# Attention beside a spectral mixing layer: the first value products of each head in runs of three key tiles

## The chip, the cores and the metric

The program runs on one core of one Trainium2 chip, in one launch. The metric is device time in microseconds (us), the median of several executions. Of the core's engines, TensorE (PE in the profile) multiplies matrices into PSUM banks, ScalarE (ACT) does exponentials and copies, VectorE (DVE) and GpSimd (POOL) do elementwise work, and SyncE (SP) issues DMAs. PEld is TensorE's loading of the stationary operand.

## The reference

Two independent parts on sequences of 2048 tokens with 448 features, their outputs side by side:

```python
# part A: Fourier mixing, real part of a DFT over features and sequence
a = einsum("bsd,ed->bse", x, dft_hid_re)
b = einsum("bsd,ed->bse", x, dft_hid_im)
y = einsum("ts,bse->bte", dft_seq_re, a) - einsum("ts,bse->bte", dft_seq_im, b)
# part B: full softmax attention, 16 heads of 28
q, k, v = split(x @ wqkv)
p = softmax(einsum("bhqd,bhkd->bhqk", q, k) * 28 ** -0.5)
o = einsum("bhqk,bhkd->bhqd", p, v) @ wo
```

Everything is float32. Both parts must be computed on one core.

## The kernel before, in words

The attention sets most of the time. For each head the 2048 keys are 16 key tiles of 128, the 2048 queries 4 chunks of 512. For a key tile and a chunk TensorE makes a 128x512 block of scores (L1302) in a PSUM bank, and ScalarE reads the bank and writes the exponential (L1310) into half of a `kept` buffer. When the exponentials of a key tile are done, `quad` (L1279) multiplies them with the values: four matmuls (L1285), one for each chunk, with a stationary operand 32 columns wide, which write four groups of 32 rows of one bank and run beside each other. The profile counts each of them twice, 8 for a key tile. A head's sum over its 16 key tiles stays in that bank, `PO[h]`, until `out_of` (L1331) has ScalarE copy it (L1337); it is then divided by the row sums.

Key tile 0 of a head is special (`first_tiles`, L1231): its scores (L1243) give a row maximum that is subtracted from all scores of the head. They are copied by ScalarE (L1247) and transposed by VectorE (L1248), and their exponential is taken in place later (L1276). This is done during the head before.

TensorE has other work in this stage: projections (L687, for the queries, keys and values of later heads) and the transforms of part A (L877). They are called filling matmuls here. They write bank 0 alone in this stage; the seven other banks are for scores, first tiles and `PO`. After the attention stands the output projection (L1470).

The order on each engine is made while the program is built. `Schedule.run` keeps a clock for the five engines and hands each free engine the ready task with the smallest key, by durations written in the kernel; a task that needs a buffer or bank is passed over until one is free. The chip then runs each engine's instructions in that fixed order, with semaphores between the engines.

`sums` (L1313) cuts the 256 value products (16 heads of 16 key tiles) into runs. The products of a run follow each other without other matmuls between. A run is ready when all its exponentials are done and when `LEAD` = 6 score matmuls behind its last key tile's have been issued. On the planner's clock a change between scores and value products costs TensorE `PE_TURN` = 0.33 us. The size of a run comes from `run_size`; before, `RUN_AT` makes it 2 for all.

Of the kernel before, what the change touches and what calls it, by code (L numbers as in the profile page):

```python
# [27 lines left out]
NC = S // CH  # L28
# [13 lines left out]
FILL_AT = 48.0, 75.0  # L42
N_WARM = 9
N_FIRST = 3
RUN_AT = ((0.0, 2),)


def run_size(t):

    return [n for at, n in RUN_AT if at <= t][-1]  # L50


SOON = 40.0
# [301 lines left out]
def tile_kernel(ctx, tc, xa, wre, wim, wd, xb, wqkv, wo, out):  # L355
# [119 lines left out]
    begins = [T_ATT + h * P_H for h in range(H)]  # L475
    dt = P_H / (NT * NC)
# [27 lines left out]
    def place(at, n):  # L504
        return big[:, at:at + n], at + n
# [4 lines left out]
    wb_all, at = place(16 * 2 * E, 8 * WB)  # L510
    wb_of = wb_all.rearrange("p (n l t) -> p n l t", n=4, l=2)
    ext_all, at = place(at, 2 * 258)
# [766 lines left out]
    def quad(h, kt, deps, key):  # L1279

        o, tiles = PO[h], R[h][kt]

        def emit(e):
            for c in range(NC):
                nc.tensor.matmul(o.t[c * VW:(c + 1) * VW, :], VT[h].t[:, kt // 4, kt % 4, :], tiles[c].t,  # L1285
                                 start=(kt == 0), stop=(kt == NT - 1))
        return pe(key, emit, d=0.2146 * NC, lat=LAT_V if kt == NT - 1 else 0.25, deps=[*deps, *got_v[h]],
                  use=[tiles[0].pair, tiles[2].pair, VT[h], o], mode=1)
# [24 lines left out]
    def sums():  # L1313
        quads = [(h, kt) for h in range(H) for kt in range(NT)]
        at, last_pv = 0, None
        while at < len(quads):
            h, kt = quads[at]
            n = run_size(begins[h] + kt * NC * dt)
            run = quads[at:at + n]
            at += n  # L1320
            h, kt = run[-1]
            key = begins[h] + (kt + 1) * NC * dt
            ahead = max(turn_at.get(i, 0) for i in run) + LEAD
            ready = in_turn[ahead - 1:ahead] + [x for i in run for x in es[i]] + [x for i in run for x in got_v[i[0]]]
            for i in run:
                last_pv = quad(*i, [*ready, last_pv], key)
                ready = []
                if i[1] == NT - 1:
                    out_of(i[0], PO[i[0]], last_pv, begins[i[0]] + P_H)

    def out_of(h, o, pv, key):  # L1331

        pair, sm = kept_s.slot(), sm_s.slot()
        osb, sbc = Half(pair, 0), Half(pair, 1)
        final = h == H - 1
        late = -60 if final else -20
        a = act(key + late, lambda: nc.scalar.activation(osb.t, o.t, AF.Copy), deps=[pv], use=[o], acq=[pair])  # L1337
        sums_of = lambda: sbc.t.rearrange("p (j r) -> p j r", r=32)[:, :, DH]
        t = dve(key + late, lambda: nc.vector.transpose(sbc.t, osb.t), 0.73, deps=[a], use=[pair])  # L1339
        r = dve(key + late, lambda: nc.vector.reciprocal(sm.t[:, 1, :], sums_of()), 0.3, deps=[t], acq=[sm], use=[pair])  # L1340
        k0 = dve(key + late, lambda: nc.vector.tensor_scalar(sm.t[:, 0, :], sums_of(), SUM_MAX, None, op0=ALU.is_le), 0.25,
                 deps=[t, r], use=[sm, pair])
        t = dve(key + late, lambda: nc.vector.transpose(sbc.t, sm.t[:, 1, :].unsqueeze(2).to_broadcast([P, NT, 32])), 0.72,  # L1343
                deps=[r, k0], use=[sm, pair])
        k1 = dve(key, lambda: nc.vector.tensor_scalar(sm.t[:, 1, :], sm.t[:, 1, :], SUM_MAX, None, op0=ALU.is_le), 0.25, deps=[t], use=[sm])
        checked.append(dve(key, lambda: nc.vector.tensor_reduce(
            ok[:, h:h + 1], sm.t.rearrange("p a b -> p (a b)"), axis=AX.X, op=ALU.min), 0.25, deps=[k1], use=[sm]))
        mul = sch.add({"POOL": 1.25, "DVE": 0.69} if final else {"POOL": 1.25}, key + late, lambda e: eng[e].tensor_tensor(  # L1348
            osb.t, osb.t, sbc.t, op=ALU.mult), deps=[t], use=[pair])
        if final:  # L1350
            ends.append((osb, mul))
            return
        for c in range(NC):
            o_done[h, c] = dma(key, lambda c=c: nc.sync.dma_start(
                on_d[h * DH:(h + 1) * DH, c * CH:(c + 1) * CH], osb.t[c * VW:c * VW + DH, :]), 56, deps=[mul], use=[pair])
# [43 lines left out]
    for h in range(H):  # L1399
        scores(h)  # L1400
    sums()
    for part in range(2):
        col = col_s.slot()
        at = CHECK_AT + 2 * part * CHECK_STEP
# [230 lines left out]
```

## Time and profile before

| | |
|---|---|
| median of 3 runs | 695.8 us (695.61 to 695.81) |
| the profiled execution | 693.96 us |
| its span, from first to last instruction | 692.4 us |
| granted TensorE clock, mean | 0.998 |
| instructions | 12770 |
| key tiles in value products | 256, in 128 runs of two |
| first and last value product starts | 67.2 and 645.6 us |

In a row of the profile a group of instructions is named by line, engine and operation, then what it writes and reads. "x960" is the count; behind the bar stand busy time, mean duration in ns, and the idle time of the engine before these instructions with what ended it. In rows in order of time the first two numbers are start and length in us, and brackets give the idle time before. Matmuls overlap in the profile, so the step from one start to the next tells what one costs.

### The profile page before, as it was taken

What the parts mean: (1) busy time and instruction counts of PE and PEld (TensorE: products, weight loads), DVE (VectorE), ACT (ScalarE), POOL (GpSimd) and SP (SyncE); (2) the same over time, 40 slices, a digit from 0 to 9 for tenths busy, and PEclk for the clock granted to TensorE, in tenths of its full rate; (3) what the DMA queues carried; (4) which work ended last, traced back from release to release, by engine and by line L of the source; (5) the groups of instructions that cost most, each with busy time, mean ns of one, the idle gap of its engine ahead of it and who ended that gap; (6) DMA issues with size and microseconds to landing.
All of it is one profiled execution on the core that took longest, in us unless ns stands there. A gap on an engine that the chain in (4) does not pass through costs nothing. (4 is left out here: it accounts for less than half of the span.)

```text
span 692.4 us, 12770 instructions
## 1 busy us (share of the span) xinstructions
PE 683.0 (99%) x4147; PEld 395.3 (57%) x4147; DVE 491.8 (71%) x857; ACT 607.7 (88%) x1233; POOL 354.8 (51%) x344
## 2 busy tenths in 40 slices
PE   8999999999999999999999999999999999999996
PEld 7897555555555555455455545555555555455786
DVE  6458639587969489698978796989697927531780
ACT  6416999999998999999999999999999999999442
POOL 8504315357545346554735564548778421545660
PEclk9999999999999999999999999999999999999999
DMA  8866789886969888989779898671443311344177
GB/s 302 282 198 208 187 213 233 215 222 209 250 175 249 214 237 236 229 238 232 217 201 248 222 249 225 185 233 59 147 145 99 101 49 52 99 133 137 34 183 243
DMA packets 101808, 131.38 MB, mean 190 GB/s; under 512 B 34231, under 2 KB 64585, under 8 KB 101733
## 3 DMA queue, kind: packets, MB, share of 16 engines
q1 hardware_dynamic: 99685, 128.62, 67.7%
q0 software_dynamic: 2048, 1.86, 1.1%
q8 instruction: 35, 0.57, 0.4%
q14 instruction: 40, 0.33, 0.2%
HBM read 100.28 MB, written 36.88 MB: 198 GB/s over the span
## 5 line engine op out<-in xcount | busy, mean ns | idle before, releaser
L1310 ACT ACTIVATE kept<-bank 128x512 f32<-128x512 f32 x960 | 506.0, 708 | 13.0 <-PE bank L1302 11.9
L1302 PE MATMUL bank<-q,k 98*128 98x512 f32 x960 | 295.7, 410 | 1.5 <-ACT kept L1310 0.8
L1285 PE MATMUL bank<-kept,v 128*32 128x512 f32 x2048 | 246.2, 598 | 0.0
L1302 PEld LDWEIGHTS bank<-q,k 98*128 98x128 f32 x960 | 171.4, 188 | 129.9 <-ACT kept L1310 92.2
L972 POOL TENSOR_TENSOR raw<-raw,raw 128x1024 f32<-128x1024 f32 (+3 forms) x57 | 107.9, 1898 | 72.3 <-DVE raw L972 37.7
L1285 PEld LDWEIGHTS bank<-kept,v 128*32 128x32 f32 x2048 | 53.4, 109 | 116.5 <-issue 110.8
L909 DVE TENSOR_REDUCE far<-raw 128x1 f32<-128x1024 f32 (+3 forms) x78 | 86.0, 1111 | 8.2 <-POOL raw L1086 4.4
L1274 POOL TENSOR_TENSOR kept<-kept,mb 128x512 f32<-128x512 f32 x41 | 58.2, 1427 | 26.5 <-DVE mb L1269 13.9
L1247 ACT ACTIVATE kept<-bank 128x512 f32<-128x512 f32 x64 | 40.3, 693 | 24.7 <-PE bank L1243 21.6
L1272 POOL CAST q<-mb 1x512 fp32r<-1x512 f32 x31 | 24.6, 808 | 69.3 <-DVE mb L1269 49.2
L1248 DVE STREAM_TRANSPOSE mb<-bank 128x512 f32<-128x512 f32 x64 | 43.6, 700 | 20.0 <-PE bank L1243 15.0
L1348 POOL TENSOR_TENSOR kept<-kept 128x512 f32<-128x512 f32 x16 | 20.9, 1304 | 59.9 <-DVE kept L1343 42.7
L1276 ACT ACTIVATE kept<-kept 128x512 f32<-128x512 f32 x64 | 49.4, 783 | 0.0
L687 PE MATMUL bank<-big,whi 128*128 128x512 f32 x132 | 46.8, 396 | 0.0
L687 PE MATMUL bank<-wd,big 128*128 128x224 f32 x288 | 43.9, 274 | 0.4 <-ACT kept L1310 0.3
L687 PEld LDWEIGHTS bank<-wd,big 128*128 128x128 f32 x288 | 40.5, 191 | 4.7 <-issue 0.8
L1269 DVE STREAM_TRANSPOSE mb<-am 128x512 f32<-128x512 f32 x62 | 41.9, 696 | 0.8
L1249 DVE TENSOR_REDUCE qm<-mb 128x16 f32<-128x512 f32 x64 | 41.5, 668 | 0.4
L972 DVE TENSOR_TENSOR raw<-raw,raw 128x1024 f32<-128x1024 f32 (+3 forms) x27 | 34.5, 1281 | 6.5 <-DMA raw<-wre 6.3
L1339 DVE STREAM_TRANSPOSE kept<-kept 128x512 f32<-128x512 f32 x16 | 11.4, 710 | 27.6 <-ACT kept L1337 27.5
L797 DVE COPY kept<-bank 128x224 f32<-128x224 f32 x32 | 12.3, 386 | 24.1 <-PE bank L687 23.8
L1272 DVE CAST q<-mb 1x512 fp32r<-1x512 f32 x31 | 27.9, 902 | 1.0
(181 smaller groups left out, 782.6 us busy)
## 6 DMA issues: line engine op xcount, KB each, us to landing
raw<-wre SPq DMA_DIRECT2D x64, 256.0 KB
raw<-wim SPq DMA_DIRECT2D x64, 256.0 KB
qkd<-kept SPq DMA_DIRECT2D x40, 256.0 KB
k<-qkd SPq DMA_DIRECT2D x64, 112.0 KB
q<-qkd SPq DMA_DIRECT2D x64, 112.0 KB
kept<-xb SPq DMA_DIRECT2D x16, 256.0 KB
vd<-kept SPq DMA_DIRECT2D x8, 512.0 KB
raw<-wre SPq DMA_DIRECT2D x32, 128.0 KB
```

Source lines behind the costliest of these rows:

```text
L687: nc.tensor.matmul(o.t[:, :cols], w(), x(), start=(i == 0), stop=(i == n - 1))
L909: far_done.append(dve(key, lambda: nc.vector.tensor_reduce(far[rows, part, n:n + 1], t(), axis=AX.X if len(t().shape) == 2 else AX.XY, op= ...
L972: return sch.add(d, at, lambda g: eng[g].tensor_tensor(xv(), xv(), yv(), op=op), deps=[*x.ld, *y.ld, *deps], use=[x.raw, y.raw])
L1248: t = dve(key, lambda o=o, tm=tm: nc.vector.transpose(tm.t, o.t), 0.73, deps=[m], acq=[tm], use=[o], lock=[o], own=RAW_S)
L1249: rs.append(dve(key, lambda tm=tm, c=c: nc.vector.tensor_reduce(qm.t[:, 0, c * NT:(c + 1) * NT], tm.t.rearrange("p (j r) -> p j r", r=32), ...
L1269: t = dve(key, lambda mb=mb, c=c: nc.vector.transpose(mb.t, f32(am.t)[:, c * NT:(c + 1) * NT].unsqueeze(2).to_broadcast([P, NT, 32])), 0.7 ...
L1272: row.append(sch.add({"DVE": 0.95, "POOL": 0.8}, key, lambda e, q=q, mb=mb: eng[e].tensor_copy(q.t[96:97, :], mb.t[96:97, :]), deps=[t], u ...
L1274: sh = sch.add({"DVE": 1.15, "POOL": 1.4}, key + (6 if h == 0 else 0), lambda e, s=s, mb=mb: eng[e].tensor_tensor(s.t, s.t, mb.t, op=ALU.add),
L1276: shown.append(act(key, lambda s=s: nc.scalar.activation(s.t, s.t, AF.Exp, scale=SCALE), ACT_S, deps=[sh], use=[s.pair]))
L1285: nc.tensor.matmul(o.t[c * VW:(c + 1) * VW, :], VT[h].t[:, kt // 4, kt % 4, :], tiles[c].t, start=(kt == 0), stop=(kt == NT - 1))
L1302: m = pe(key, lambda e, o=o, q=q, kt=kt: nc.tensor.matmul(o.t, KT[h][kt // 4].t[:KM, kt % 4 * P:(kt % 4 + 1) * P], q.t[:KM, :], start=True ...
L1310: es[h, kt].append(act(key - 20, lambda o=o, p=p: nc.scalar.activation(p.t, o.t, AF.Exp, scale=SCALE), deps=[m], use=[o, p.pair]))
```

## The change

`run_size` now takes the number of the run's first key tile in the head instead of a time, and reads the run's length from a tuple: 3, 3, 2, 2, 2, 2, 2. So key tiles 0 to 2 and 3 to 5 of each head are runs of three, the other ten are five runs of two: 7 runs a head instead of 8, 112 instead of 128.

```diff
-RUN_AT = ((0.0, 2),)
-
-
-def run_size(t):
-
-    return [n for at, n in RUN_AT if at <= t][-1]
+RUNS = (3, 3, 2, 2, 2, 2, 2)
+
+
+def run_size(kt):
+
+    return next(n for i, n in enumerate(RUNS) if sum(RUNS[:i]) == kt)
...
-            n = run_size(begins[h] + kt * NC * dt)
+            n = run_size(kt)
```

The planner then orders all engines anew. In the orders below an L1285 row is two of a key tile's four matmuls, so two rows are a key tile; numbers behind the names are buffers. First TensorE at the change from the seventh to the eighth head in the kernel before: the end of the piece behind the seventh head's last run, the eighth head's first run (sum in bank 4), and the next matmul.

```order
L1302 MATMUL bank1_123<-q6_98,k2_87 128x512
L1243 MATMUL bank5_127<-q0_92,k1_86 128x512
L1302 MATMUL bank6_128<-q7_99,k2_87 128x512
L1302 MATMUL bank2_124<-q3_95,k2_87 128x512
L1302 MATMUL bank3_125<-q4_96,k2_87 128x512
L1285 MATMUL bank4_126<-kept15_115,v1_91 32x512 x2
L1285 MATMUL bank4_126<-kept13_113,v1_91 32x512 x2
L1285 MATMUL bank4_126<-kept12_112,v1_91 32x512 x2
L1285 MATMUL bank4_126<-kept4_104,v1_91 32x512 x2
L1243 MATMUL bank1_123<-q1_93,k1_86 128x512
```

The same place with the change: the last rows of the piece, the first run (sum in bank 1), and the next matmul.

```order
L1302 MATMUL bank2_124<-q7_99,k2_87 128x512
L687 MATMUL bank0_122<-big_68,whi_83 128x512
L1302 MATMUL bank6_128<-q3_95,k4_89 128x512
L687 MATMUL bank0_122<-big_68,wlo_84 128x512
L1302 MATMUL bank3_125<-q4_96,k4_89 128x512
L1285 MATMUL bank1_123<-kept6_106,v1_91 32x512 x2
L1285 MATMUL bank1_123<-kept9_109,v1_91 32x512 x2
L1285 MATMUL bank1_123<-kept12_112,v1_91 32x512 x2
L1285 MATMUL bank1_123<-kept14_114,v1_91 32x512 x2
L1285 MATMUL bank1_123<-kept13_113,v1_91 32x512 x2
L1285 MATMUL bank1_123<-kept10_110,v1_91 32x512 x2
L1243 MATMUL bank5_127<-q2_94,k1_86 128x512
```

Before, four scores of L1302 and one first tile stand between the two heads' runs, and no filling matmul. With the change there are eight, two first tiles and four filling matmuls. Up to the second run there were then eight more scores, and are now twelve.

ScalarE at the same place, from the copy of the seventh head's sum on, before:

```order
L1337 ACTIVATE kept14_114<-bank7_129 128x512
L1310 ACTIVATE kept5_105<-bank2_124 128x512
L1310 ACTIVATE kept5_105<-bank3_125 128x512
L1247 ACTIVATE kept2_102<-bank5_127 128x512
L1247 ACTIVATE kept2_102<-bank1_123 128x512
L1310 ACTIVATE kept7_107<-bank6_128 128x512
```

And with the change:

```order
L1337 ACTIVATE kept5_105<-bank6_128 128x512
L1310 ACTIVATE kept2_102<-bank3_125 128x512
L1310 ACTIVATE kept2_102<-bank1_123 128x512
L1310 ACTIVATE kept3_103<-bank5_127 128x512
L1310 ACTIVATE kept3_103<-bank2_124 128x512
L1310 ACTIVATE kept4_104<-bank6_128 128x512
L1310 ACTIVATE kept4_104<-bank3_125 128x512
L1247 ACTIVATE kept0_100<-bank4_126 128x512
L1247 ACTIVATE kept0_100<-bank7_129 128x512
L1247 ACTIVATE kept7_107<-bank5_127 128x512
```

The copies of first tiles (L1247) have moved behind all six scores that TensorE issues ahead of the run of three; the third of them reads the first matmul behind that run.

## The prediction

> **What bounds the kernel now.** I read the page first (busy shares, slices, costliest groups), then the busy time by stage, then TensorE's and ScalarE's rows in order of time around single runs of value products.
>
> ```profile
> PE 683.0 (99%) x4147; PEld 395.3 (57%) x4147; DVE 491.8 (71%) x857; ACT 607.7 (88%) x1233; POOL 354.8 (51%) x344
> ACT  6416999999998999999999999999999999999442
> PEclk9999999999999999999999999999999999999999
> L1310 ACT ACTIVATE kept<-bank 128x512 f32<-128x512 f32 x960 | 506.0, 708 | 13.0 <-PE bank L1302 11.9
> L1302 PE MATMUL bank<-q,k 98*128 98x512 f32 x960 | 295.7, 410 | 1.5 <-ACT kept L1310 0.8
> L1285 PE MATMUL bank<-kept,v 128*32 128x512 f32 x2048 | 246.2, 598 | 0.0
> ```
>
> Two engines are candidates. TensorE (PE) is busy in 99% of the span at a full granted clock, and ScalarE (ACT) in nine tenths of every slice of the attention. Busy shares cannot part them, because matmuls overlap in the profile (410 ns each, though they start closer together, below) and so do the exponentials (708 ns). By stage:
>
> ```profile
> core 0: us, PE busy (x) PEld busy (x) DVE busy (x) ACT busy (x) POOL busy (x), PEclk, DMA share, GB/s
> 100.00:600.00 500.00, 498.91 (x3027) 259.64 (x3020) 397.61 (x627) 486.18 (x982) 273.68 (x235) 1.00 0.71 189
> 646.00:692.40 46.40, 40.81 (x227) 37.22 (x223) 25.77 (x62) 14.66 (x36) 20.03 (x23) 0.98 0.63 172
> PE bank L1302 <- DVE mb L1248: 0.5, 1, 0.5
> PE bank L1302 <- ACT kept L1310: 0.5, 1, 0.5
> L1285 PE MATMUL bank<-kept,v x2048: 592/592/617, 67.2 to 645.6; 128*32 128x512 f32 x187
> ```
>
> In 500 us of attention TensorE has 1.1 us without a matmul, and the two waits that the profile names for it sum to 1.0 us. The value products reach from 67.2 to 645.6 us: 578.4 us for 16 heads, so 36.2 us a head. Now the same for ScalarE:
>
> ```profile
> 326.46 6.69 ACT L1310 ACTIVATE kept<-bank 128x512 f32<-128x512 f32 x13 [0.51 <-PE bank L1302]
> 335.45 4.03 ACT L1310 ACTIVATE kept<-bank 128x512 f32<-128x512 f32 x8 [0.34 <-PE bank L1302]
> 339.29 0.70 ACT L1276 ACTIVATE kept<-kept 128x512 f32<-128x512 f32 x1
> 339.81 4.09 ACT L1310 ACTIVATE kept<-bank 128x512 f32<-128x512 f32 x8
> 343.63 0.78 ACT L1276 ACTIVATE kept<-kept 128x512 f32<-128x512 f32 x1
> ```
>
> Eight exponentials from 339.81 to 343.63 are 0.478 us each from start to start, and an exponential in place (L1276) is 0.52. The 982 activations between 100 and 600 us are then about 472 us of 500: ScalarE has some 28 us free there, 2.0 us a head. Its idle time stands behind scores (L1302), which arrive late after a run of value products. So TensorE sets the pace, and ScalarE is only 5 to 6% behind it.
>
> **What one run costs.** First matmuls around one run in order of time, then its weight loads:
>
> ```profile
> 217.26 0.39 PE L687 MATMUL bank<-big,whi 128*128 128x512 f32 x1
> 217.49 0.42 PE L1302 MATMUL bank<-q,k 98*128 98x512 f32 x1
> 217.85 1.92 PE L1285 MATMUL bank<-kept,v 128*32 128x512 f32 x16
> 219.70 0.50 PE L1302 MATMUL bank<-q,k 98*128 98x512 f32 x1
> 220.04 0.40 PE L687 MATMUL bank<-big,whi 128*128 128x512 f32 x1
> 220.27 0.39 PE L1302 MATMUL bank<-q,k 98*128 98x512 f32 x1
> ```
>
> ```profile
> 217.84 0.16 PEld L1285 LDWEIGHTS bank<-kept,v 128*32 128x32 f32 x8 [0.25 <-issue]
> 218.30 0.13 PEld L1285 LDWEIGHTS bank<-kept,v 128*32 128x32 f32 x4 [0.30 <-issue]
> 218.73 0.13 PEld L1285 LDWEIGHTS bank<-kept,v 128*32 128x32 f32 x4 [0.30 <-issue]
> 219.70 0.19 PEld L1302 LDWEIGHTS bank<-q,k 98*128 98x128 f32 x1 [0.84 <-DVE qm L1255]
> ```
>
> A plain matmul follows the one before by 0.23 us (217.26 to 217.49, 220.04 to 220.27). Into the run the step is 0.36 instead of 0.23, the run takes 1.85 (217.85 to 219.70), and the first step after it is 0.34 instead of 0.23. Inside the run the products of one key tile are two groups of four weight loads; groups follow each other by 0.43 us (218.30 to 218.73), so a key tile is 0.86 us and two are 1.72. What a run costs beyond its products is therefore 0.13 ahead, 1.85 - 1.72 = 0.13 inside and 0.11 behind, 0.37 us. In many other runs the step in is about 0.33, so I take 0.35 us a turn, as an estimate between 0.33 and 0.37.
>
> **The change, part by part.**
> - Removed: 16 of the 128 runs, 16 x 0.35 = 5.6 us of TensorE, all between 67.2 and 645.6 us where TensorE is never free. It is on the path that sets the end.
> - Unchanged: all matmuls, exponentials and transfers, and the rows of TensorE behind the last run, which stand in the same order as before (bank numbers aside). The 46 us behind 646 us therefore move as they are.
> - Moved: the first run of a head now stands 14 score matmuls into the head instead of 10, the second 26 instead of 18; then both kernels have runs at 34, 42, 50, 58 and 66. The short piece before, in which only four scores of L1302 stood between the last run of a head and the first of the next, is gone (now eight, then twelve). Moving the other matmuls (projections and transforms that fill between) costs nothing in itself: TensorE does them anyway, and no product of the attention uses them at once.
> - Added: in 32 places ScalarE gets no scores for one key tile longer, 0.86 us. A run of three lasts 1.85 + 0.86 = 2.71 us, and the next score takes some 0.4 us more until it can be read. Of eight banks one is for the filling matmuls and one holds the sum, so at most six scores lie ready, 6 x 0.478 = 2.87 us of work. ScalarE will run dry behind most of these runs, by my count for about 1 us where it now stands for 0.3 to 0.5 (the two rows above). That costs TensorE nothing at once: an empty queue means that every bank is free again.
> - The possible cost is in the pieces between: ten and fourteen scores (products for the next head's first tiles, L1243, counted in) at 0.23 us are faster than ScalarE's 0.478, and the seventh unread score makes TensorE wait. At the change from the seventh to the eighth head I followed the orders of both engines by hand with the steps above (both are shown with the change). ScalarE first empties the old sum's bank (L1337), then two copies of first tiles (L1247) are left to do while the run of three goes on, which covers part of the dry time. Four and seven filling matmuls stand between the scores, so ten scores take 3.3 us and fourteen 4.9 us. Each reused bank has been read about 0.4 us before its matmul comes. No wait there.
> - In the order of one head, the seventh, no filling matmul stands ahead of either run of three. Fifteen scores then come in 3.5 us, ScalarE takes (3.5 - 0.5) / 0.478 = 6 of them, and 9 are left where 6 fit: 3 x 0.478 = 1.4 us of waiting. The other heads have 4 to 20 filling matmuls ahead of the second run.
>
> How large these waits are in all, no row of before shows for runs of three. Bounds: below, -1.0 us, if the two named waits at head changes go with the short piece; above, the larger of them, 0.52 us, at each of the 32 runs, 16.6 us. I take +0.6 us: the seventh head's 1.4 us, less most of the 1.0 us of the short pieces. That is near the lower end, where the hand-followed head stands.
>
> Sum: -5.6 + 0.6 = -5.0 us. The profiled execution took 693.96 us (span 692.4), 1.8 under the median of 695.8. On its scale the result is 689.0, on the median's 690.8.
>
> **The rivals.**
> - *Part of the gain comes back.* The mechanism is the same, but TensorE waits in many heads instead of one, 0.1 us on average before or after each run of three: 32 x 0.1 = 3.2, net -2.4, 693.4 us. For it speaks that ScalarE's free time falls to 2.0 - 0.35 = 1.65 us a head, while two dry stretches of up to 1 us each want more; against it, that ScalarE starts every piece with empty banks, so nothing it has missed can pile up over two pieces.
> - *ScalarE is the bound, and nothing happens.* The 486 us busy of 500 speak for it, the 1.1 us of free TensorE against. If ScalarE paced the stage, TensorE's saved turns would come back as waits on banks one for one: 695.8 us. The Trainium skill ("Perfetto Trace Analysis", Identifying the Most-Contended Engine) warns that busy time of matmuls is a poor measure and has TensorE judged by its weight loads; by that the ranking here is ACT 88% over PEld 57%, and the sum would be zero. The trace does not agree: from start to start TensorE leaves no gaps, ScalarE does.
> - *The longer run makes it slower.* TensorE meets a full set of banks in the crowded pieces ahead of a run of three, and each such wait is of the size seen now, 0.52 us. It decides from 5.6 / 32 = 0.17 us a run; at half of the 32 places it is 16 x 0.52 - 5.6 = +2.7, 698.5 us, at all 706.8. The named waits of now, 1.0 us in 500, speak against it, the thin margin of 0.4 us for it. The skill ("TensorEngine Tiling (Array Packing)", PSUM Bottleneck) says that products packed by columns shift the load to the reading of PSUM; no run here shows yet how far.
> - That the change does not do what it says is out: the order has 112 runs, two of three key tiles at the head of each group of seven.
>
> **How the numbers follow.** Chances: forecast 0.60 (690.8, its own range 689 to 692.5), part of the gain 0.14, nothing 0.13, slower 0.13. About 0.2% (1.4 us) is what can be told from no change, so faster is 0.60 + 0.14 = 0.74. The lower end of the range is all turns and the two named waits gone: -5.6 - 1.0, some 0.4 more for the price of a turn at 0.37: 688.8. The upper end takes in the case without effect: 695.9; it leaves out the slower case and a little below.
>
> **What would show it.** In the profile after: 112 value runs, those of three about 2.71 us from first product to next score, first value product some 1 us later, the last about 5 us earlier than 645.6; TensorE's free time between 100 and 600 us still about 1 to 2 us; single ScalarE gaps of up to 1 us behind the runs of three. Wrong would be: TensorE waiting for L1310 or L1248 dozens of times (rivals one or three), or a run of three longer than 2.71 us, because its third tile costs more than 0.86 us.

## The result and the profile after

| | before | after |
|---|---|---|
| median | 695.79 us (695.61 to 695.81, 4 runs) | 706.19 us (705.15 to 708.44, 4 runs) |
| ratio, 95% interval | 1 | 1.0145 (1.0122 to 1.0167) |
| the profiled execution, its span | 693.96, 692.4 us | 708.44, 706.9 us |
| runs of value products | 128 | 112 |
| first and last value product start | 67.2, 645.6 us | 69.1, 657.5 us |

The kernel became 10.4 us slower; 5.0 us faster was forecast. From the page of after, the busy shares, the clock slices and the three groups that were shown of before:

```profile
span 706.9 us, 12765 instructions
PE 691.4 (98%) x4147; PEld 401.2 (57%) x4147; DVE 500.8 (71%) x862; ACT 607.8 (86%) x1234; POOL 349.8 (49%) x338
PEclk9999999999999999899999999999999999999999
L1310 ACT ACTIVATE kept<-bank 128x512 f32<-128x512 f32 x960 | 506.2, 730 | 21.3 <-PE bank L1302 20.2
L1302 PE MATMUL bank<-q,k 98*128 98x512 f32 x960 | 306.3, 415 | 5.7 <-ACT kept L1310 3.2
L1285 PE MATMUL bank<-kept,v 128*32 128x512 f32 x2048 | 244.8, 602 | 0.0
```

The share column again shows a full TensorE, 98% for 99%, though there is 14 us more to explain. The idle columns moved: ScalarE stands 20.2 us behind scores instead of 11.9, and TensorE 3.2 instead of 0.8 us ahead of scores until ScalarE has read a bank. Both engines wait more, each for the other. Then the busy time of 500 us of attention, and what TensorE waits for there (us in total, times, longest us):

```profile
100.00:600.00 500.00, 494.45 (x2948) 259.37 (x2947) 396.12 (x617) 474.36 (x959) 257.16 (x216) 0.99 0.70 187
PE bank L1302 <- ACT kept L1310: 2.4, 5, 0.7
PE bank L1302 <- DVE q L1272: 1.7, 2, 1.1
PE bank L1302 <- DVE mb L1248: 0.8, 2, 0.6
```

The number in brackets is the better measure, though it counts wide and narrow matmuls alike. TensorE started 3027 matmuls in this stretch before, and 2948 now. That is 2.6% fewer, where busy time fell by 0.9%: matmuls overlap in the records, so a late start of a few tenths makes the overlap smaller before it makes a gap.

For the same reason I summed, over all pairs of neighbouring matmuls between the first and the last value product and outside the value runs, what the step from start to start lasts beyond the plain step of that shape (0.23 us for 512 columns). Before, these late starts sum to 6.3 us, 26 of them over 0.1 us. After they sum to 20.4 us (17.3 at full clock, 52 over 0.1 us; 3.1 in two short stretches at half clock, below). The two profiled executions then differ like this:

| term | us |
|---|---|
| first value product later (69.1 for 67.2) | +1.9 |
| 16 turns fewer, 0.35 each | -5.6 |
| late starts between matmuls, 20.4 for 6.3 | +14.1 |
| a run of three at half clock, 4.63 for 2.71 | +1.9 |
| from the last value product to the end, 49.3 for 46.7 | +2.6 |
| sum; the spans differ by 14.5 | +14.9 |

The profiled execution of after lies 2.3 us above its median and that of before 1.8 us below, so 14.5 us in the spans stand for 10.4 in the medians.

The place where it is seen best is the seventh head, which the prediction named. TensorE's rows in order of time, and ScalarE's from 288.68 us on:

```profile
285.43 2.78 PE L1285 MATMUL bank<-kept,v 128*32 128x512 f32 x24
288.14 0.96 PE L1243 MATMUL bank<-q,k 84*128 84x512 f32 x3
288.95 0.84 PE L1302 MATMUL bank<-q,k 98*128 98x512 f32 x3
290.31 0.99 PE L1302 MATMUL bank<-q,k 98*128 98x512 f32 x2 [0.52 <-ACT kept L1310]
291.49 3.49 PE L1302 MATMUL bank<-q,k 98*128 98x512 f32 x7 [0.18 <-DVE mb L1248]
294.91 4.70 PE L1285 MATMUL bank<-kept,v 128*32 128x512 f32 x24
299.54 0.50 PE L1302 MATMUL bank<-q,k 98*128 98x512 f32 x1
```

```profile
288.68 1.09 ACT L1247 ACTIVATE kept<-bank 128x512 f32<-128x512 f32 x2 [0.36 <-PE bank L1243]
289.65 1.09 ACT L1310 ACTIVATE kept<-bank 128x512 f32<-128x512 f32 x2
290.61 0.65 ACT L613 ACTIVATE whi<-raw 128x512 fp32r<-128x512 f32 x1
291.13 5.03 ACT L1310 ACTIVATE kept<-bank 128x512 f32<-128x512 f32 x10
295.89 0.75 ACT L1247 ACTIVATE kept<-bank 128x512 f32<-128x512 f32 x1
300.08 0.60 ACT L1310 ACTIVATE kept<-bank 128x512 f32<-128x512 f32 x1 [3.43 <-PE bank L1302]
```

Behind the first run of three (24 rows, 285.43 to 288.14 = 2.71 us) fifteen scores and first tiles follow without a filling matmul. Six of them start at once; the seventh waits until ScalarE has freed a bank, and from 288.14 to 294.91 the fifteen take 6.77 us instead of 3.5 (the last of them at half clock). ScalarE is then the busy engine, and 1.7 us into the next run of three it has done all that is ready and stands for 3.43 us. The second run lasts 299.54 - 294.91 = 4.63 us, because the clock fell, and that lengthens the dry time too. The same two steps, TensorE ahead of itself and then ScalarE dry, appear smaller in other heads, and in the third head the engine waited for is VectorE, which writes the row maximum that the next scores need (L1272; rows of other work are left out):

```profile
166.24 1.19 PE L1302 MATMUL bank<-q,k 98*128 98x512 f32 x4
168.52 0.47 PE L1302 MATMUL bank<-q,k 98*128 98x512 f32 x1 [1.09 <-DVE q L1272]
170.84 0.93 PE L1302 MATMUL bank<-q,k 98*128 98x512 f32 x3 [0.64 <-DVE q L1272]
```

By the last value product of each head, measured from that of the head before, the longest additions are the seventh (+4.5 us, with 6.8 us of half clock), the third (+3.8) and the fourteenth (+2.1, half clock); seven of the fifteen steps are shorter than before, by 0.4 us on average, where 0.35 was to be saved.

### The profile page after: what moved, and what is told of

Read it like the earlier page. It is cut to its first block, busy times and chain, and to the rows that moved or that the text cites. A ratio compares the mean times of both kernels' runs of the same rounds, so it can differ in the third digit from the quotient of the medians.

```text
span 706.9 us, 12765 instructions
## 1 busy us (share of the span) xinstructions
PE 691.4 (98%) x4147; PEld 401.2 (57%) x4147; DVE 500.8 (71%) x862; ACT 607.8 (86%) x1234; POOL 349.8 (49%) x338
## 5 line engine op out<-in xcount | busy, mean ns | idle before, releaser
L1310 ACT ACTIVATE kept<-bank 128x512 f32<-128x512 f32 x960 | 506.2, 730 | 21.3 <-PE bank L1302 20.2
L1302 PE MATMUL bank<-q,k 98*128 98x512 f32 x960 | 306.3, 415 | 5.7 <-ACT kept L1310 3.2
L1302 PEld LDWEIGHTS bank<-q,k 98*128 98x128 f32 x960 | 173.8, 189 | 132.0 <-ACT kept L1310 93.7
L1285 PE MATMUL bank<-kept,v 128*32 128x512 f32 x2048 | 244.8, 602 | 0.0
L1285 PEld LDWEIGHTS bank<-kept,v 128*32 128x32 f32 x2048 | 55.4, 110 | 120.9 <-issue 117.1
L1274 POOL TENSOR_TENSOR kept<-kept,mb 128x512 f32<-128x512 f32 x43 | 59.9, 1404 | 23.9 <-DVE mb L1269 15.7
L1247 ACT ACTIVATE kept<-bank 128x512 f32<-128x512 f32 x64 | 42.4, 748 | 28.7 <-PE bank L1243 27.1
L1272 POOL CAST q<-mb 1x512 fp32r<-1x512 f32 x28 | 21.8, 783 | 65.6 <-DVE mb L1269 30.9
L972 DVE TENSOR_TENSOR raw<-raw,raw 128x1024 f32<-128x1024 f32 (+3 forms) x31 | 39.5, 1277 | 12.2 <-DMA raw<-wre 11.5
L1272 DVE CAST q<-mb 1x512 fp32r<-1x512 f32 x34 | 29.8, 884 | 1.0
L687 PEld LDWEIGHTS bank<-big,whi 128*128 128x128 f32 x132 | 24.7, 189 | 5.9 <-issue 0.8
L710 DVE TENSOR_TENSOR kept<-bank,kept 128x512 fp32r<-128x512 f32 x20 | 13.3, 687 | 20.6 <-ACT kept L709 18.2
```

The lines of the kernel that those rows point to most:

```text
L687: nc.tensor.matmul(o.t[:, :cols], w(), x(), start=(i == 0), stop=(i == n - 1))
L972: return sch.add(d, at, lambda g: eng[g].tensor_tensor(xv(), xv(), yv(), op=op), deps=[*x.ld, *y.ld, *deps], use=[x.raw, y.raw])
L1247: made.append(act(key, lambda o=o, s=s: nc.scalar.activation(s.t, o.t, AF.Copy), deps=[m], use=[o, s.pair], lock=[o]))
L1272: row.append(sch.add({"DVE": 0.95, "POOL": 0.8}, key, lambda e, q=q, mb=mb: eng[e].tensor_copy(q.t[96:97, :], mb.t[96:97, :]), deps=[t], u ...
L1274: sh = sch.add({"DVE": 1.15, "POOL": 1.4}, key + (6 if h == 0 else 0), lambda e, s=s, mb=mb: eng[e].tensor_tensor(s.t, s.t, mb.t, op=ALU.add),
L1302: m = pe(key, lambda e, o=o, q=q, kt=kt: nc.tensor.matmul(o.t, KT[h][kt // 4].t[:KM, kt % 4 * P:(kt % 4 + 1) * P], q.t[:KM, :], start=True ...
```

## The experiments

Three explanations stood against each other. *Starved ScalarE*: a run of three leaves ScalarE dry, the scores must be caught up in the piece between, and TensorE stands for banks that ScalarE has not read. *New order*: the runs are harmless, but the planner ordered all five engines anew, and this order is worse. *Cover*: the runs cost only where no filling matmuls lie ahead of them. In the recorded expectations the first is theory 1, the second theory 2; a theory 3, that a run of three is slow in itself, stands beside them, and its median of 2.71 us, as forecast, speaks against it. Each experiment is compared with the kernel before on the same chip (medians 696.6 to 697.6 us); the ratios are to those runs.

**A fast ScalarE.** The exponential of the scores covers the left 256 of 512 columns only, with the planner told so; what is left out is the right half's exponentials. Once with runs of two (e1), once with the change's runs (e2).

```diff
-                es[h, kt].append(act(key - 20, lambda o=o, p=p: nc.scalar.activation(p.t, o.t, AF.Exp, scale=SCALE),
-                                     deps=[m], use=[o, p.pair]))
+                es[h, kt].append(act(key - 20, lambda o=o, p=p: nc.scalar.activation(p.t[:, :CH // 2], o.t[:, :CH // 2], AF.Exp, scale=SCALE),
+                                     0.3, deps=[m], use=[o, p.pair]))
```

> Runs of two as before, but the exponential of the scores (L1310) reads and writes only the left 256 of 512 columns, so the right halves of the probability tiles keep old values; the planner reckons 0.30 us for it. ScalarE then has some 10 us a head to spare. Theory 1 (banks: behind and ahead of a run of three, TensorE waits for banks that ScalarE has not read) says this kernel is close to before, since TensorE set its pace there: 689 to 696 us. Theory 2 (any new order loses against the old one) says 698 to 704.

> The changed kernel (two runs of three at the head of each head) with the same half exponential. Theory 1: with ScalarE fast the waits on banks shrink, and the 16 saved turns show: 2 to 6 us faster than the run of twos with half exponentials. Theory 2 and a theory 3 (a run of three is slow in itself): still 4 to 11 us slower than it.

Measured: e1 0.9972 (0.9953 to 0.9990), 694.6 us; e2 0.9958 (0.9927 to 0.9989), 693.9 us. The groups of e1 and e2, exponentials, and the attention's 500 us of each:

```profile
L1310 ACT ACTIVATE kept<-bank 128x256 f32<-128x256 f32 x960 | 296.4, 403 | 163.0 <-PE bank L1302 161.1
100.00:600.00 500.00, 496.57 (x3025) 261.96 (x3025) 398.32 (x627) 329.91 (x987) 264.65 (x227) 1.00 0.71 189
```

```profile
L1310 ACT ACTIVATE kept<-bank 128x256 f32<-128x256 f32 x960 | 293.7, 410 | 149.9 <-PE bank L1302 140.0
100.00:600.00 500.00, 496.25 (x3047) 264.27 (x3043) 405.27 (x631) 329.55 (x990) 275.17 (x235) 1.00 0.72 190
```

With ScalarE busy 330 of 500 us the same change no longer costs 10 us: the medians differ by -0.8 us, which is within the noise of the two ratios. Runs of three are not harmful in themselves; they cost where ScalarE has little slack. e1 is also a new order of runs of two, since the planner had another duration to reckon with, and it lost nothing either. The expected gain of 2 to 6 us of e2 over e1 is not seen in the medians; runs of e2 spread from 687.9 to 697.7 us. First to last value product the profiles give 577.2 us (e1) and 572.2 us (e2), 5.0 us less, and 3047 matmuls in the 500 us for 3025. But the profile of e1 has 3.4 us at half clock in this stretch (140.3 to 143.7 us), worth at most 1.7 us, and that of e2 has none, so about 3.3 us are left for the change, where 5.6 us of turns were saved; late starts at full clock grew by 3.6 us here too.

**Which heads.** `run_size` gets the head too. In e3 the nine heads with few, half-wide or no filling matmuls ahead of their runs of three have them; in e4 the other seven.

```diff
+RUNS, TWOS = (3,3,2,2,2,2,2), (2,) * 8
+LONG = (0,1,2,4,6,12,13,14,15,)   # e4: (3,5,7,8,9,10,11,)
...
+    runs = RUNS if h in LONG else TWOS
+    return next(n for i, n in enumerate(runs) if sum(runs[:i]) == kt)
```

> Runs 3, 3, 2, 2, 2, 2, 2 only in the nine heads in which the fillers are half as wide, few or none (the 1st, 2nd, 3rd, 5th, 7th and 13th to 16th); twos in the others. Theory 1: nearly the whole loss of the change, 702 to 707 us. Theory 2 or 3: about nine sixteenths of it, 700 to 702.

> Runs 3, 3, 2, 2, 2, 2, 2 only in the seven heads where full-width fillers (0.23 us each) stand ahead of the second run (the 4th, 6th and 8th to 12th); twos in the others. Theory 1: fourteen runs of three save seven turns and cost little, -2.5 to +2 us against before, 693 to 698. Theory 2 or 3: 699 to 701.

Measured: e3 1.0119 (1.0080 to 1.0157), 705.5 us; e4 1.0064 (1.0041 to 1.0086), 701.1 us. The covered heads lose 4.5 us as well, where a gain was expected. Each kernel has a new order too, which alone cost 4.4 us on average in four others (below); less that, e3 would lose 4 us and e4 nothing. So the direction fits, the expected gain of e4 is missing, and one order of each is too few to decide on cover.

**A new order of the old runs.** Runs of two; one duration in the planner (its default for an operation of VectorE) 0.70 instead of 0.69 us, which is enough to send it another way.

```diff
-ACT_P, ACT_S, DVE_P, POOL_2, SMALL = 0.48, 0.52, 0.69, 1.25, 0.36
+ACT_P, ACT_S, DVE_P, POOL_2, SMALL = 0.48, 0.52, 0.70, 1.25, 0.36
```

> Runs of two everywhere, as before. Only the planner's duration for a VectorE pass is 0.70 instead of 0.69 us, so all engines are ordered anew with nothing else changed. Theory 1 (banks): within 3 us of before, 693 to 699. Theory 2 (any new order loses): 700 to 706.

Measured: 1.0064 (1.0039 to 1.0089), 702.6 us. With none of the change in it the kernel lost 4.5 us, more than theory 1 allowed. TensorE's waits of e5 in the 500 us:

```profile
100.00:600.00 500.00, 496.14 (x2975) 256.38 (x2974) 402.95 (x618) 478.69 (x966) 267.73 (x222) 1.00 0.72 187
PE bank L1302 <- DVE mb L1248: 2.5, 1, 2.5
PE bank L1302 <- ACT kept L1310: 1.0, 3, 0.4
```

**Other places and sizes.** Runs of three in the middle of the head, 2, 2, 3, 3, 2, 2, 2 (e6); shorter runs at its ends, 1, 2, 2, 2, 2, 2, 2, 2, 1 (e7).

> Runs 2, 2, 3, 3, 2, 2, 2: the two runs of three moved from the head change to key tiles 4 to 9. Theory 1 says that any run of three leaves ScalarE dry and crowds the piece behind it: 700 to 708 us. A theory 1b, that only the head change is too crowded (first tiles and two sums hold banks there), says 689 to 694.

> Runs 1, 2, 2, 2, 2, 2, 2, 2, 1: nine a head, 144 instead of 128, the other way round. If a turn costs TensorE 0.35 us as the rows said, and shorter runs relieve the banks a little: +2 to +6 us, 698 to 702. If the price of a turn was wrong (nothing on the path): 694 to 697.

Measured: e6 1.0165 (1.0142 to 1.0188), 709.3 us, a little above the expected range: runs of three in the middle of a head lose as well, so a crowded change of heads is not needed for the loss. e7 1.0078 (1.0047 to 1.0109), 701.9 us; the planner let neighbouring runs touch, and the trace has 134 runs rather than 144, so it is no clean price of a turn: six turns are 2.1 us, and the rest of the 5.4 is of the size that new orders cost by themselves below, which this run does not show separately.

**A few runs of three.** Runs of three in three heads alone, 125 runs in all (e8).

```diff
+TWOS = (2,) * 8
+RUNS = {15: (2, 2, 2, 2, 2, 3, 3), 4: (3, 3, 2, 2, 2, 2, 2), 10: (3, 2, 2, 2, 2, 2, 3)}
...
```

> Runs of three in three heads only: 3, 3, 2, 2, 2, 2, 2 in the fifth, 3, 2, 2, 2, 2, 2, 3 in the eleventh, 2, 2, 2, 2, 2, 3, 3 in the last. Theory 1: three turns saved at little cost, -0.5 to -2 us, 693.5 to 695.3. Theory 2: +2 to +6.

Measured: 0.9974 (0.9959 to 0.9989), 695.0 us for 697.3. This one is faster than before, by 1.8 us (0.8 to 2.9), where three turns are 1.05. Its 500 us, and its exponentials:

```profile
100.00:600.00 500.00, 499.10 (x3030) 260.42 (x3029) 404.13 (x628) 486.12 (x984) 270.72 (x234) 1.00 0.72 189
L1312 ACT ACTIVATE kept<-bank 128x512 f32<-128x512 f32 x960 | 507.3, 727 | 13.9 <-PE bank L1304 13.1
```

3030 matmuls, and ScalarE's idle time behind scores is 13.1 us, near the 11.9 of before. Late starts sum to 6.7 us. So a new order need not cost: outside the value products TensorE's is that of before for its first 781 of 2099 matmuls and another behind. Nearness to the old order alone does not explain it, since e13 (below) keeps to it for 603, differs less behind that, and is slower than before.

**The old order with the new runs.** Every engine's order of before is written down as a table; only the value products are gathered into 3, 3, 2, ... (e9).

```diff
+ORDER = [...]     # for each engine the numbers of its tasks, from the kernel before
...
+                    if at_[e] == len(order[e]) or t.n != order[e][at_[e]]:
+                        aside.append(item)
+                        continue
...
```

> No re-planning: every engine keeps the order of before from a table, and only the value products of TensorE are regrouped to 3, 3, 2, 2, 2, 2, 2, the first run behind score 14 and the second behind score 26 of each head. Theory 2 (runs of three are harmless, the new order loses): 688 to 693 us, the 16 turns saved. Theory 1 (the longer run drains ScalarE's banks and crowds them again): slower than before and than the change, since the fillers no longer move into the crowded pieces: 708 to 725 us.

Measured: 1.0318 (1.0284 to 1.0353), 720.5 us. In its trace all other matmuls and all of ScalarE's work stand in the order of before. Its exponentials (L1441 here; the scores are L1433) and TensorE's waits in the 500 us:

```profile
L1441 ACT ACTIVATE kept<-bank 128x512 f32<-128x512 f32 x960 | 511.1, 724 | 38.8 <-PE bank L1433 37.4 <-issue 1.0
100.00:600.00 500.00, 495.80 (x2896) 251.15 (x2896) 373.54 (x596) 466.87 (x943) 260.65 (x219) 1.00 0.71 186
PE bank L1433 <- ACT kept L1441: 1.7, 5, 0.6
```

ScalarE's idle time behind scores is three times that of before, and 2896 matmuls start instead of 3027. Harmless runs in a bad new order would have made this kernel faster; it lost 23 us. The new order repairs more than half of what runs of three do to the old one.

**Pairs: twos and threes, both ordered anew.** Since a new order can cost by itself, the change has to be compared with twos that were also ordered anew. e12 is e5 with runs of three. Three more pairs change one planner constant each: `SLACK` (time that the planner leaves for DMAs to land) 5.0 to 4.0, `LAT_V` (until a head's sum can be read) 1.3 to 1.2, `T_FILL` (when the pace of the filling matmuls ends) 665 to 660.

> The changed kernel with 0.70 us for a VectorE pass in the planner; its twos were run before (+4.5 us against before). Theory 1: 4 to 11 us slower than those twos, +8 to +15 against before. Theory 2: within 3 us of them, +2 to +7 against before.

> A pair with the next: runs of two, the planner reckons 4.0 instead of 5.0 us of slack for landing DMAs (SLACK), so the order is new. Theory 2: 699 to 704 us, like the other new order of twos (+4.5 us). Theory 1 with some luck of the order on top: 694 to 700.

> The changed kernel with SLACK 4.0. Theory 1: 4 to 11 us slower than its twos. Theory 2: like its twos, within 3 us, or up to 5.6 us faster.

> A pair with the next: runs of two, the planner reckons 1.2 instead of 1.3 us until the last value product of a head can be read (LAT_V), so the order is new. If every new order of twos loses some 4.5 us, as two have: 699 to 704. If the old order is only one of several good ones: 694 to 699.

> The changed kernel with LAT_V 1.2. If runs of three cost some 3 us for any order of the rest, as two pairs say: 2 to 5 us slower than its twos. If the 10 us of the change are their cost: 8 to 12 slower than its twos.

> A pair with the next: runs of two, the pace of the filling matmuls ends 5 us earlier (T_FILL 660), so the order is new. If every new order of twos loses some 4.5 us: 699 to 704. Else 694 to 699.

> The changed kernel with T_FILL 660. Some 3 us for the runs of three: 2 to 5 us slower than its twos; 10 us: 8 to 12 slower.

| constant | twos, 95% | threes, 95% | difference |
|---|---|---|---|
| as in the change | 1 | 1.0145 (1.0122 to 1.0167) | +1.45% |
| `DVE_P` 0.70 (e5, e12) | 1.0064 (1.0039 to 1.0089) | 1.0105 (1.0073 to 1.0137) | +0.41% |
| `SLACK` 4.0 (e10, e11) | 1.0064 (1.0038 to 1.0089) | 1.0111 (1.0066 to 1.0156) | +0.47% |
| `LAT_V` 1.2 (e13, e14) | 1.0049 (1.0021 to 1.0076) | 1.0117 (1.0071 to 1.0162) | +0.68% |
| `T_FILL` 660 (e15, e16) | 1.0075 (1.0042 to 1.0108) | 1.0167 (1.0122 to 1.0212) | +0.92% |

Two things are separate now. All four new orders of the unchanged runs are slower than before, by 0.63% on average, 4.4 us: the old order is a favourable one among these neighbours. And in all four pairs threes are slower than twos, by 0.62% on average, 4.3 us, net of the turns that they save. One pair alone would hardly show it: in three of the four the intervals overlap. By the ratios the first two gave 2.9 and 3.3 us, where theory 1 expected 4 or more; the last two gave 4.7 and 6.4, where 2 to 5 was expected.

The late starts in the profiles show where this comes from. They sum to 6.3 us before; at full clock to 10.3 to 12.7, mean 11.1, in the four new orders of twos; to 14.4 to 17.4, mean 16.4, in those of threes; and to 17.3 in after. So of the 11 us of late starts that the change added at full clock about 5 came with the new orders and about 5 with the runs of three. By the semaphore that came last before each late start, ScalarE's exponentials (L1310) ended 4.3 us of them before, 6.2 on average in the new orders of twos, 9.9 in those of threes, 9.0 in after, and 19 of 31 us in e9. Most of what the runs of three added is waiting for banks that ScalarE had not read.

These 5.3 us about cancel the 5.6 us of saved turns. From first to last value product the profiles of threes take only 0.7 us longer than their twos (-0.2 to +1.9); in e12 as many matmuls start in the 500 us as in e5 (2975):

```profile
100.00:600.00 500.00, 495.58 (x2972) 259.34 (x2974) 400.43 (x622) 477.18 (x965) 257.30 (x224) 0.99 0.72 188
```

The spans of threes are 2.9 us longer on average, and the other 2.1 us are a first value product that starts 1.5 us later and an end that is 0.7 us longer. The profiled executions of twos lie 0.8 us above their medians on average and those of threes 0.6 us below, which makes up the 4.3 us.

## Why the prediction was wrong

- **Removed turns: right.** 112 runs stand in the trace. The steps into and out of a run and inside it lose 0.104, 0.105 and 0.13 us more than plain ones in after too, 0.34 a turn and 5.4 us in all, for 0.35 and 5.6. What failed is that other waits took their place.
- **Length of a run of three: right.** The median of the 32 is 2.71 us.
- **ScalarE dry for about 1 us behind each: right** (0.95 on average, as the longest step from start to start beyond 0.48 us), and "costs TensorE nothing at once" too. The failing step is the next one.
- **"The possible cost", +0.6 us: wrong, by more than a factor of 20.** This is the step that failed. It was the waits of one head less those of the short pieces; the profile has 14 us of late starts more, about 5 of them from the new order (next point). Four things failed in it. I followed one quiet head by hand (the eighth, where no loss showed later either) and let it stand for all others but one. I held that ScalarE "starts every piece with empty banks, so nothing it has missed can pile up over two pieces": inside one piece of ten to fifteen scores the unread ones fill the six banks, which is where TensorE then waits. The prediction had this rule (the seventh unread score) and worked it out for two heads of sixteen. The seventh head's 1.4 us was seen but came as 4.5 us, VectorE's delay and the half clock included. And the cost was looked for in the named waits (1.0 us in 500), where 6.3 us of late starts already lay hidden beneath overlapping matmuls.
- **"Moving the other matmuls costs nothing in itself": wrong.** It holds for TensorE's own work, but the order is that of five engines. Runs of two in four new orders lose 3.4 to 5.2 us (0.49 to 0.75% of 696), and a part of the added late starts are waits for VectorE that moved, as in the third head. No row of before could have given this figure; that an order is made anew should have stood in the sum as an unknown with both signs.
- **"The 46 us behind 646 us move as they are": wrong by 2.6 us.** Two waits show part of it, VectorE's for output buffers and TensorE's for VectorE. Before, then after:

```profile
662.26 0.63 DVE L470 COPY kept<-bank 128x448 f32<-128x448 f32 x1 [0.68 <-DMA out<-kept]
670.11 3.87 PE L1470 MATMUL bank<-wd,q 128*128 128x448 f32 x18 [0.37 <-DVE q L458]
```

```profile
676.97 0.62 DVE L470 COPY kept<-bank 128x448 f32<-128x448 f32 x1 [3.11 <-DMA out<-kept]
684.27 3.99 PE L1470 MATMUL bank<-wd,q 128*128 128x448 f32 x18 [1.44 <-DVE q L458]
```

  TensorE's order is the same there; the other engines' was made anew. The four new orders of twos have tails of 48.7 to 49.3 us as well.
- **First value product some 1 us later:** 1.9 us.
- **The rivals.** The third, "the longer run makes it slower", had the mechanism, at a chance of 0.13. That its time with all 32 places, 706.8, comes out is luck: its waits were not 0.52 us at each run but many smaller ones and a few long ones, and about half of the loss is the new order, which no rival had. That ScalarE is the bound was half right: its slack of 28 us in 500 decides what a change on TensorE may do, as e1 and e2 show, and between orders made alike (the pairs) the saved turns did come back as late starts almost one for one. Against the old order the time grew beyond that. The Trainium skill ("TensorEngine Tiling (Array Packing)", PSUM Bottleneck) says that after such packing the copying out of PSUM may become the bottleneck. No run here shows that by itself, since the products are packed alike in both kernels; e2 shows only that a faster reader of the banks removes the loss.

What stays open: the split (of 1.45%, 10.1 us: 4.4 for the order, 4.3 for the runs, 1.4 for neither) rests on four pairs that spread from 2.9 to 6.4 us, and why the order of before, or that of e8, is good where its neighbours are not was not found.

## What to carry to other kernels

Where a second engine is only some 5% behind the first and a handful of banks lie between them, a saving on the first is worth what the second's slack allows inside each piece between two stops, not on average over the stage; set the longest stretch without feed against the work that the banks hold, and the piece behind it against the second engine's rate, for every place and not for one. Where a planner orders everything anew, compare the change with several re-ordered versions of the unchanged kernel, since one good order may lose more than the change is worth. And read steps from start to start beside the busy share: a TensorE at 98 to 99% hid 20 us of late starts.

## What the runs showed of the hardware

TensorE's granted clock fell to half in the middle of the attention, in after from 292.0 to 298.8 us and from 554.8 to 558.2 us. For each, the 3 us ahead and the stretch itself, then 3 us of the third head behind which the clock stayed full (the clock stands third from the end):

```profile
289.00:292.00 3.00, 2.30 (x8) 1.07 (x6) 3.00 (x5) 3.00 (x7) 2.23 (x2) 1.00 0.99 197
292.00:298.80 6.80, 6.80 (x26) 2.36 (x29) 3.50 (x5) 4.64 (x10) 3.54 (x5) 0.50 0.91 220
551.80:554.80 3.00, 2.34 (x10) 1.39 (x10) 2.29 (x7) 2.87 (x8) 0.84 (x2) 1.00 0.32 74
554.80:558.20 3.40, 3.40 (x12) 3.02 (x13) 3.40 (x7) 2.83 (x7) 1.13 (x2) 0.50 0.03 7
165.70:168.70 3.00, 1.91 (x13) 0.89 (x6) 2.94 (x7) 3.00 (x8) 3.00 (x3) 1.00 0.94 252
```

Ahead of the first, 8 matmuls started in 3 us at full clock, where 13 plain ones fit, and TensorE was busy for 2.30 us; no single wait in these 3 us or ahead of the second exceeds 0.66 us. Before had no such stretch until its last matmul was done; three profiles of other kernels with runs of two (e1, e5, e15) had, so it does not belong to runs of three. The Trainium skill ("TensorE: Matmul & The Clock Gate", A second HAM failure mode: psum-queue depth-cycling) tells of short idle times between matmuls, from cycling through PSUM banks, that bring the half clock on; the two stretches of after agree, but the third head's 3 us, with TensorE busy for only 1.91, passed without it, so how much idle time it takes is not shown here. Small waits can cost twice: a run of three took 4.63 us instead of 2.71. It is the smaller part here, though: the four runs of after have mean clocks of 0.991 to 0.997, and the fastest, 705.15 us at 0.997, is still 9.4 us above before.
